# Loading eight decay rates as a column and spreading them over the partitions by a TensorE transpose

## The chip, the cores and the metric

The kernel runs on one core of one Trainium2 chip. A core has a matrix engine (TensorE, PE in the profile), a vector engine (VectorE, DVE), an activation engine (ScalarE, ACT), a general engine (GpSimd, POOL) and a queue engine (SyncE, SP), each with an instruction stream of its own; they meet through semaphores. SBUF and PSUM have 128 partitions, and TensorE writes only into PSUM. The metric is device time in microseconds, the median of several runs; lower is better.

## The reference

A gated linear attention over four sequences of 768 tokens with eight heads is followed by a mixture of eight experts that picks one expert for each token. Only the first part concerns the change:

```python
Dmask = np.where(rel >= 0, lam[:, None, None] ** rel[None, :, :], 0.0)
lam_pow = lam[:, None, None] ** (pos[None, :, None] + 1)
...
intra = np.einsum('bhic,bhjc->bhij', qb, kb) * Dmask[None]
intra = np.einsum('bhij,bhjd->bhid', intra, vb)
inter = np.einsum('bhid,bhde->bhie', qb * lam_pow[None], kv_state)
out[:, :, sl] = intra + inter
rev_pow = lam[:, None, None] ** (block - 1 - pos[None, :, None])
kb_dec = kb * rev_pow[None]
kv_state = lam_block[None, :, None, None] * kv_state + np.einsum('bhsd,bhse->bhde', kb_dec, vb)
```

`lam` holds eight numbers, one decay rate to a head. Everything that the attention multiplies by is a power of them: the causal mask, the powers for the queries, and the reversed powers for the keys. The second part scores each token for the experts and, where a local gate says so, lets it keep its predecessor's expert; then `out = p[e] * relu(x @ w1[e]) @ w2[e]`.

## The kernel before

The attention takes 24 steps, one for each of six chunks of 128 tokens in each of four sequences (`ORDER`, the sequences inside). Step s works on a tile `inp[s]` of 128 partitions by 4 by 512 numbers: transposed queries, transposed keys, values and keys. Six such tiles are held at a time (`LOADS`). The first five are loaded in halves (queries and keys, then values and keys) on SP's queue, in the order tile 0 first half, tile 1 first half, tile 0 second half, tile 1 second half, then both halves of tiles 2 to 4. Later tiles are loaded whole, once TensorE has read the last of the tile six steps before.

A step has these parts. `scores(s)` (L212, or L204 in some steps) multiplies keys by queries into `ps` on TensorE; DVE multiplies the result by `mask` into `sm` (L216). From the second chunk on `from_state(s)` (L239) applies the carried state `kv` to `qd`, queries times powers, which POOL made (L181). `mix(s)` (L252) multiplies values by `sm`, and ACT copies the result to `xc` (L255). `update(s)` (L266) multiplies `kd`, keys times reversed powers, made by POOL (L184), by the values; DVE adds it to `kv` (L269, L271). Between these stand the routing of earlier tokens and the writes of finished rows.

The experts' part follows. It begins with three tiles of 128 tokens that are already known, and then takes the experts one after the other, with TensorE products on weights that SP loads ahead.

The order on TensorE, DVE, SP and POOL is that of the code (`tc.manual_schedule`); ACT's instructions at the start are ordered by a scheduler.

At the very start, `lamb` (L104) is loaded on ACT's queue: each of the 128 partitions gets a copy of all eight rates, read 128 times from DRAM. POOL builds the identity matrix `ident`. TensorE does ten warming products of `ident` with itself, whose result is not used (L874, `WARM`). `masks_of_lam` makes the powers. `spread` (L131) writes one rate into each of 127 columns of a piece, for the even heads on DVE and for the odd heads on ACT; two scans on DVE (L146) multiply along the columns, restarted by ones that come from `ident`, and give `mask`; `rev` (L149) is a column of it. The query powers `lamq` come later from a third spread on ACT and two more scans (L159).

Of the kernel before, what the change touches and what calls it, by code (L numbers as in the profile page):

```python
# [8 lines left out]
F32 = mybir.dt.float32  # L9
# [14 lines left out]
P = 128  # L24
B, H, S, DH = 4, 8, 768, 64
A = H // 2
DM = H * DH
# [13 lines left out]
QUARTERS = [16, 17, 18, 19]  # L41
WIDE = [3, 4, 5, 7, 9, 11]
TURNED = {**{r: r + 1 for r in range(3 * B)}, 11: 13, 20: 22, 21: 23, 22: 23}
WARM = 10
KA = 3
assert KA <= -(-(NA * P - E * (P - 1)) // P)

# [21 lines left out]
def kernel(  # L69
# [9 lines left out]
    nc = tc.nc  # L79
    const = ctx.enter_context(tc.tile_pool(name="const", bufs=1))  # L80
# [19 lines left out]
        return w2[bass.ds(e, 1)].rearrange("o (t p) d -> p (o t) d", p=P)  # L100


    lamb = const.tile([P, H], F32, name="lamb")
    nc.scalar.dma_start(out=lamb, in_=lam.unsqueeze(0).broadcast_to([P, H]))  # L104
    wgt = const.tile([P, DT, EP], F32, name="wgt")
    ident = const.tile([P, P], F32, name="ident")
    make_identity(nc, ident)
# [2 lines left out]

    pg = ctx.enter_context(tc.tile_pool(name="pg", bufs=1, space=PSUM))
    x_ctx = ExitStack()
    load = x_ctx.enter_context(tc.tile_pool(name="load", bufs=LOADS))
    att = x_ctx.enter_context(tc.tile_pool(name="att", bufs=2))
    pows = x_ctx.enter_context(tc.tile_pool(name="pows", bufs=1))
# [754 lines left out]
    with tc.manual_schedule(engines={PE, DVE, SP, POOL}):  # L870

        warm = pg.tile([P, A, P], F32, name="pk0")
        for _ in range(WARM):
            nc.tensor.matmul(warm[:, 0], lhsT=ident, rhs=ident, start=True, stop=True)  # L874
        masks_of_lam()
        nc.gpsimd.memset(wgt, 0.0)
# [453 lines left out]
    with tc.manual_schedule(engines={PE, DVE, SP, ACTE}):  # L1330
        last, i = KA - 1, (KA - 1) % 2
# [121 lines left out]
```

## Time and profile before

| what | before |
|---|---|
| median of 3 runs | 416.93 us (415.94 to 417.92) |
| the profiled execution's own time | 416.13 us |
| its span, first to last instruction | 414.4 us |
| instructions | 10134 |
| PE / DVE / ACT / POOL busy | 96% / 75% / 52% / 44% |
| moved by DMA | 90.69 MB, mean 219 GB/s |
| warming products (L874) | 1.96 to 6.59 us |
| issue of `lamb`, first use of it | 0.82 us, 5.93 us |

Rows of the profile read as follows. In a timeline a row gives the start, the length, the engine, the line, the operation, the tile written and those read, shapes (partitions by elements), the count of entries that were merged, and in brackets the idle time before it with what ended it. "PEld" is the loading of TensorE's stationary operand; "SPq" and "ACTq" are queues that issue DMAs. One product of 32-bit numbers is two entries on TensorE. In a row of DMA queues stand packets, megabytes and the share of the 16 DMA engines' time; q1 is SP's queue, q10 ACT's. In a row of stretches stand the stretch, its length, each engine's busy time (PE, PEld, DVE, ACT, POOL), the granted TensorE clock, the DMA share and GB/s. In a row of groups stand the count, the busy time in us, and the mean of one in ns.

### The profile page before, as it was taken

The page shows a single profiled execution, that of the slowest core. Times are in us where ns is not written, and L with a number is a line of the kernel's source. Part 1 is how long each engine was busy: PE and PEld are TensorE (multiplying, and loading weights), DVE is VectorE, ACT ScalarE, POOL GpSimd, SP SyncE. Part 2 cuts the span into 40 slices and gives each one's busy share as a digit, 9 for nine tenths or more (in the row PEclk, how much of TensorE's full clock was granted, in tenths as well). Part 3 has the DMA queues.
Part 4 walks back from the last instruction along what each step waited for, and adds up shares of the span by engine and source line. Part 5 has one row for each costly group of instructions (what it writes and reads, how often), then busy time and mean ns, then how long its engine had stood idle before and what let it go on. Part 6 is the DMA issues. An engine that isn't in the chain of part 4 may idle for free. (4 is left out here: it accounts for less than half of the span.)

```text
span 414.4 us, 10134 instructions
## 1 busy us (share of the span) xinstructions
PE 397.0 (96%) x3970; PEld 363.4 (88%) x3970; DVE 309.3 (75%) x573; ACT 214.7 (52%) x646; POOL 184.2 (44%) x188
## 2 busy tenths in 40 slices
PE   7999979889999989999999999999999999999994
PEld 6778868667786769989999999999999999999983
DVE  4676987887667797897797786787967868676931
ACT  4245546432931856925944946764674493652210
POOL 4585665440016210147257238617527713700752
PEclk9999999999999999999999999999999999999999
DMA  7999999999987993563464453725617535200111
GB/s 266 404 390 331 361 408 276 331 382 407 355 312 282 361 359 137 219 220 125 197 223 131 173 186 115 270 78 190 235 52 240 179 137 174 96 11 2 43 35 62
DMA packets 36585, 90.69 MB, mean 219 GB/s; under 512 B 3808, under 2 KB 11504, under 8 KB 34608
## 3 DMA queue, kind: packets, MB, share of 16 engines
q1 hardware_dynamic: 30080, 74.47, 49.6%
q0 software_dynamic: 5152, 13.38, 9.7%
q10 hardware_dynamic: 1296, 2.10, 1.3%
q8 instruction: 33, 0.54, 0.5%
q14 instruction: 24, 0.20, 0.1%
HBM read 81.55 MB, written 12.91 MB: 228 GB/s over the span
## 5 line engine op out<-in xcount | busy, mean ns | idle before, releaser
L1122 POOL DMA_INDIRECT out_dram<-yq,sidxq x80 | 93.4, 1167 | 102.5 <-DVE yq L1117 68.1
L1074 PE MATMUL ps<-arena,s 128*128 128x148 f32 (+7 forms) x384 | 63.4, 308 | 2.1 <-DVE part L1240 0.8
L1074 PEld LDWEIGHTS ps<-arena,s 128*128 128x128 f32 x384 | 57.2, 190 | 3.2 <-DVE part L1240 1.2
L777 POOL DMA_INDIRECT xg<-x_dram,gidx x27 | 31.7, 1174 | 55.1 <-DVE xlast L791 16.4
L798 ACT COPY arena<-xlast 32x128 f32<-32x128 f32 x128 | 37.8, 295 | 8.8 <-DVE xlast L791 6.2
L1074 PE MATMUL ps<-arena,w 128*128 128x148 f32 (+7 forms) x256 | 41.9, 307 | 0.0
L1074 PE MATMUL po<-arena,w 128*128 128x148 f32 (+7 forms) x256 | 41.9, 307 | 0.0
L1074 PEld LDWEIGHTS ps<-arena,w 128*128 128x128 f32 x256 | 38.3, 190 | 0.5 <-issue 0.5
L1074 PEld LDWEIGHTS po<-arena,w 128*128 128x128 f32 x256 | 38.2, 190 | 0.0
L216 DVE TENSOR_TENSOR sm<-ps,mask 128x512 f32<-128x512 f32 x46 | 29.4, 680 | 11.2 <-PE ps L212 6.5
L181 POOL TENSOR_TENSOR qd<-inp,lamq 128x512 f32<-128x512 f32 x20 | 25.5, 1277 | 26.4 <-DMA inp<-in_qkv_dram 10.7
L798 ACT COPY arena<-lg 32x128 f32<-32x128 f32 x120 | 35.5, 296 | 2.6
L1112 PE MATMUL pk<-h,w 128*128 128x148 f32 (+6 forms) x224 | 35.1, 310 | 0.0
L1112 PE MATMUL pk<-hsum,s 128*128 128x148 f32 (+6 forms) x224 | 35.1, 310 | 0.0
L1112 PEld LDWEIGHTS pk<-hsum,s 128*128 128x128 f32 x224 | 33.4, 190 | 0.0
L1112 PEld LDWEIGHTS pk<-h,w 128*128 128x128 f32 x224 | 33.4, 190 | 0.0
L252 PE MATMUL po<-sm,inp 128*64 128x128 f32 x384 | 27.8, 280 | 1.4 <-DVE sm L216 0.6
L252 PEld LDWEIGHTS po<-sm,inp 128*64 128x64 f32 x384 | 21.0, 136 | 9.1 <-issue 5.9
L1093 ACT COPY arena<-xlast 32x128 f32<-32x128 f32 x88 | 26.8, 305 | 1.9
L243 ACT ACTIVATE kv<-kv,lamq 128x64 f32<-128x64 f32 x64 | 17.1, 336 | 19.7 <-PE po L239 19.2
L184 POOL TENSOR_TENSOR kd<-inp,rev 128x512 f32<-128x512 f32 x20 | 21.8, 1094 | 9.4 <-DVE rev L149 4.7
L255 ACT COPY xc<-po 128x256 f32<-128x256 f32 x48 | 15.6, 375 | 17.8 <-PE po L252 16.7
(296 smaller groups left out, 750.8 us busy)
## 6 DMA issues: line engine op xcount, KB each, us to landing
w<-in_w_dram SPq DMA_DIRECT2D x23, 2048.0 KB, 9.2
inp<-in_qkv_dram SPq DMA_DIRECT2D x15, 1024.0 KB, 10.8
inp<-in_qkv_dram SPq DMA_DIRECT2D x10, 512.0 KB, 8.1
x_dram<-w SPq DMA_DIRECT2D x12, 256.0 KB, 5.5
inp<-in_qkv_dram SPq DMA_DIRECT2D x4, 768.0 KB, 9.1
x_dram<-xn ACTq DMA_DIRECT2D x8, 256.0 KB, 5.6
w<-in_w_dram SPq DMA_DIRECT2D x4, 512.0 KB, 8.3
out_dram<-yq,sidxq POOLq DMA_INDIRECT x80, 3.1
```

The source lines that it names most:

```text
L181: nc.gpsimd.tensor_tensor(qd, x[:, 0].rearrange("p (a i) -> p a i", i=P), lamq, ALU.mult)
L184: nc.gpsimd.tensor_tensor(kd.rearrange("p (h d) -> p h d", d=DH), x[:, 3].rearrange("p (h d) -> p h d", d=DH), rev.unsqueeze(2).broadcast_ ...
L216: nc.vector.tensor_tensor(sm[:, u], ps[u], mask[:, u], ALU.mult)
L243: nc.scalar.mul(kv[:, a], kv[:, a], lamq[:, a, P - 1:P])
L252: nc.tensor.matmul(head(a, u), lhsT=vn[:, a, u], rhs=sm[:, u, a], start=(not c and a < 2), stop=True, skip_group_check=True)
L255: nc.scalar.copy(xc[:, i::2, b], po[i])
L777: nc.gpsimd.indirect_dma_start(out=xg, out_offset=None, in_=x_dram[:n, :], in_offset=bass.IndirectOffsetOnAxis(ap=gidx[i][:, j:j + 1], axi ...
L798: copy((xt(k) if callable(xt) else xt)[QP * j:QP * j + QP, :, at(k):at(k) + QP], blocks[QP * k:QP * k + QP, :, j])
L1074: nc.tensor.matmul(to[:, j], lhsT=a[:, k, P * m:P * m + P], rhs=b[:, k], start=(new and not j and not k), stop=(k == 1), skip_group_check= ...
L1093: nc.scalar.copy(xu[QP * j:QP * j + QP, u % 2::2 - u % 2, :, P + QP // 2 * k:P + QP // 2 * k + QP // 2], blocks[QP * k:QP * k + QP, :, j]. ...
L1112: nc.tensor.matmul(to[:, m], lhsT=a[:, f, P * m:P * m + P], rhs=b[:, f], start=(new and not m and not f), stop=(f == FT // 2 - 1), skip_gr ...
L1122: last = nc.gpsimd.indirect_dma_start(out=out.rearrange("n (j d) -> (n j) d", j=4), out_offset=bass.IndirectOffsetOnAxis(ap=sidxq[:, u, i, ...
```

## The change

The rates are loaded as a column, `lamc`: eight partitions with one number each. `lamb` becomes the first eight columns of a bank in PSUM. TensorE fills it with one transpose: `lamc`, repeated over 128 columns, against an 8 by 8 identity gives every partition all eight rates. The warming products are five instead of ten, and the transpose stands after the second of them.

```diff
-WARM = 10
+WARM = 5
+EARLY = 2
...
-    lamb = const.tile([P, H], F32, name="lamb")
-    nc.scalar.dma_start(out=lamb, in_=lam.unsqueeze(0).broadcast_to([P, H]))
+    lamc = const.tile([H, 1], F32, name="lamc")
+    nc.scalar.dma_start(out=lamc, in_=lam.unsqueeze(1))
...
+    lamb = pg.tile([P, DM], F32, name="pk1")[:, :H]
...
         warm = pg.tile([P, A, P], F32, name="pk0")
-        for _ in range(WARM):
+        for i in range(WARM):
+            if i == EARLY:
+                nc.tensor.transpose(lamb, lamc.broadcast_to([H, P]), ident[:H, :H])
             nc.tensor.matmul(warm[:, 0], lhsT=ident, rhs=ident, start=True, stop=True)
```

Line numbers after the change are two to four higher. On TensorE the program begins as follows, before; `pk_158` is the bank of the warming products, `ps_111` and `ps_112` receive the first scores:

```order
L1449 UNCONDITIONAL_BRANCH
L874 MATMUL pk_158<-ident 128x128 x10
L212 MATMUL ps_111<-inp 64x128
L212 MATMUL ps_112<-inp 64x128
L212 MATMUL ps_111<-inp 64x128
```

And now, with `pk_89` the bank that holds the rates and `pk_159` that of the warming products:

```order
L1453 UNCONDITIONAL_BRANCH
L878 MATMUL pk_159<-ident 128x128 x2
L877 MATMUL pk_89<-ident,lamc 128x8
L878 MATMUL pk_159<-ident 128x128 x3
L214 MATMUL ps_112<-inp 64x128
L214 MATMUL ps_113<-inp 64x128
```

The transpose stands between the second and the third warming product, and it waits for the load of `lamc`; the first scores follow after three more products. Behind them TensorE's order is as it was.

On ACT the program begins as follows, before:

```order
L104 DMA lamb<-in_lam_dram 128x8
L131 ACT_TABLE_LOAD
L131 COPY w_1_77<-lamb 128x4x127
L152 COPY lamp<-lamb 64x4 x2
L131 COPY w_1_77<-lamp 128x4x127
L154 COPY w_1_77<-lamp 128x4
L361 CAST identb<-ident 128x128
L373 CAST dupq<-ident 128x512
L359 CAST count<-w_1_77 128x32
L360 CAST whole<-w_1_77 128x32
L365 CAST countb<-w_1_77 128x128
L368 CAST beforeb<-w_1_77 128x128
```

And now:

```order
L105 DMA lamc<-in_lam_dram 8x1
L363 ACT_TABLE_LOAD
L363 CAST identb<-ident 128x128
L361 CAST count<-w_1_77 128x32
L362 CAST whole<-w_1_77 128x32
L367 CAST countb<-w_1_77 128x128
L133 COPY w_1_77<-pk_89 128x4x127
L154 COPY lamp<-pk_89 64x4 x2
L370 CAST beforeb<-w_1_77 128x128
L133 COPY w_1_77<-lamp 128x4x127
L156 COPY w_1_77<-lamp 128x4
L371 CAST parts<-whole 128x24
```

Four casts of constants now stand ahead of ACT's spread. The spread reads PSUM, and in the built program it waits for DVE's spread, which reads the same bank, where it waited for the load before. DVE's order is unchanged but for its spread, which reads `pk_89` instead of `lamb` and waits for TensorE instead of the load. POOL's and SP's orders are unchanged.

## The prediction

> **What bounds the kernel now.** The page's busy shares come first, then the last pieces of the span, then its first 25 us.
>
> ```profile
> PE 397.0 (96%) x3970; PEld 363.4 (88%) x3970; DVE 309.3 (75%) x573; ACT 214.7 (52%) x646; POOL 184.2 (44%) x188
> 407.22 1.89 PE L1079 MATMUL pk<-w,hsum 128*128 128x256 f32 x8
> 409.15 0.42 DVE L1200 TENSOR_TENSOR s<-pk,s 128x256 f32<-128x256 f32 x1 [1.30 <-PE pk L1079]
> 409.85 0.98 POOL L827 DMA_INDIRECT out_dram<-s,sidx  x1 [0.74 <-POOLq L1402]
> ```
>
> TensorE (PE) is busy for 96% of the span, and the end is its last product, one VectorE (DVE) addition and the scatter. Whatever moves TensorE's whole program earlier moves the end. The change touches only the start, so the question is how much earlier TensorE gets through it, and whether that lead survives.
>
> ```profile
> 0.82 6.53 SPq L882 DMA_DIRECT2D inp<-in_qkv_dram  x10
> 0.82 0.40 ACTq L104 DMA_DIRECT2D lamb<-in_lam_dram  x1
> 1.96 4.63 PE L874 MATMUL pk<-ident 128*128 128x128 f32 x20 [1.96 <-POOL ident masks.py:199]
> 5.93 0.61 ACT L131 COPY w<-lamb 128x508 f32<-128x508 f32 x1 [3.38 <-DMA lamb<-in_lam_dram]
> 5.93 0.42 DVE L131 COPY w<-lamb 128x508 f32<-128x508 f32 x1 [3.40 <-DMA lamb<-in_lam_dram]
> 6.39 2.34 DVE L146 TENSOR_TENSOR_SCAN mask<-w 128x512 f32<-128x512 f32 x2
> 6.53 1.78 PE L212 MATMUL ps<-inp 64*64 64x128 f32 x32
> 8.76 0.17 DVE L149 COPY rev<-mask 128x8 f32<-128x8 f32 x1
> 8.84 1.28 DVE L216 TENSOR_TENSOR sm<-ps,mask 128x512 f32<-128x512 f32 x2
> 9.02 2.04 POOL L184 TENSOR_TENSOR kd<-inp,rev 128x512 f32<-128x512 f32 x2 [4.68 <-DVE rev L149]
> 9.58 0.43 PE L252 MATMUL po<-sm,inp 128*64 128x128 f32 x2 [0.40 <-DVE sm L216]
> ```
>
> Two chains meet at 8.84, the first `sm`. The mask chain: the decay rates land at 5.93, then spread copy, two scans, `rev`: 2.91 us. The score chain: ten warming products (20 entries, two to a product) hold TensorE until about 6.5, then scores(0) runs to 6.53 + 1.78 = 8.31. The mask is later by half a microsecond, and TensorE then stands idle for `sm` until 9.58. So **the rates' landing at 5.93 is what ends last here**, and the warming products are second by only 0.5 us: an edit that takes away one without the other would be worth no more than that.
>
> From there on the steps hang together without slack:
>
> ```profile
> 15.92 1.16 PE L204 MATMUL ps<-inp 64*128 64x128 f32 x16
> 17.11 1.29 DVE L216 TENSOR_TENSOR sm<-ps,mask 128x512 f32<-128x512 f32 x2 [0.73 <-PE ps L204]
> 17.90 1.64 PE L252 MATMUL po<-sm,inp 128*64 128x128 f32 x16 [0.21 <-issue]
> ```
>
> Scores, mask product, mix, next scores: each starts when the one before ends. A lead at 8.84 is handed on from step to step.
>
> **The change, part by part.** *The load.* `lamb` was 128 rows of eight numbers; `lamc` is eight rows of one. When would it land?
>
> ```profile
> DMA to landing us min/median/max: 5.1/5.1/5.1
> q10 hardware_dynamic: 144, 0.00, 2.1%
> q10 hardware_dynamic: 34, 0.00, 1.3%
> q1 hardware_dynamic: 180, 0.67, 74.6%
> q1 hardware_dynamic: 374, 1.37, 103.1%
> ```
>
> The first row is `lamb`. The next two count packets on ACT's queue (q10), from 2.25 to 5.5 us and from 2.25 to 3.5; the last two count SP's queue (q1), from 2.25 to 5.5 and from 5.5 to 8.75. All 144 packets of `lamb` (128 rows and 16 more) had gone by 5.5, and it landed 0.4 later. Eight rows are at most one per DMA engine, so `lamc` is over after about the first two rounds of 16 packets, which had gone by 3.5. Estimate: 3.5 + 0.4 = **3.9**. Bounds: 3.3, if the first round is enough; 5.9, if a landing in this crowded start takes the time that `lamb` took whatever its size. I take 3.9, since the packets of q10 were spread evenly over the time and the landing followed the last of them.
>
> *The transpose.* It stands behind two warming products, which end at 1.96 + about 0.95 = 2.9, so it waits for `lamc`; behind it in TensorE's queue wait three warming products and scores(0), and nothing else of TensorE's can pass. Its duration is not in the trace; the nearest rows:
>
> ```profile
> L874 PE MATMUL pk<-ident 128*128 128x128 f32 x20 | 4.6, 429 | 2.0 <-POOL ident masks.py:199 2.0
> L454 PE MATMUL pr<-identb,run 4*128 4x4 bf16 x6 | 0.6, 166 | 0.0
> L787 DVE COPY xt<-pr 128x512 f32<-128x512 f32 x1 | 0.7, 692 | 0.1
> ```
>
> Between 0.17 (a tiny product, later on) and 0.43 (a warming one); it is narrow but runs at the slow early pace, so I take 0.35 with the signal. The rates stand in PSUM at 3.9 + 0.35 = **4.25**.
>
> *The mask chain.* DVE's spread now reads PSUM: the copy out of `pr` costs 0.69 for 512 columns, against 0.42 from SBUF: +0.27. The scans and `rev` are as before, so `sm` can start 2.91 + 0.27 = 3.18 after 4.25, at **7.43**. ACT's spread now waits for DVE's instead of running beside it: 4.25 + 0.69 + 0.61 = 5.55, and the second scan, which needs it, starts at about 4.25 + 0.7 + 1.17 = 6.1. Hidden with 0.5 to spare; without that cover it would cost up to 0.6. ACT's constant casts are shuffled around its spread, and their cover is the time in which ACT idled before its first `xc` copy:
>
> ```profile
> 11.09 0.65 ACT L255 COPY xc<-po 128x256 f32<-128x256 f32 x2 [1.28 <-PE po L252]
> ```
>
> That copy moves up with mix(0); so does the spread ahead of it, and the 1.28 stays.
>
> *The score chain.* Three warming products are six entries at (4.63 - 0.42) / 19 = 0.22: 1.33, from 4.25 to 5.6. Scores(0) then also needs the first half tile of q and k:
>
> ```profile
> q1 hardware_dynamic: 145, 0.56, 68.0%
> q1 hardware_dynamic: 293, 1.10, 77.6%
> inp<-in_qkv_dram SPq DMA_DIRECT2D x1, 512.0 KB, 6.6
> ```
>
> Its 144 packets (128 rows and 16) had gone by 5.1 (first row: 1.75 to 5.1); the second half tile's, 288 in all, by 6.4 (second row). It landed about 0.6 later, so the first is there at about 5.7, perhaps sooner without q10's packets. Scores(0): 5.7 + 1.78 = **7.5**. The two chains meet again, mask 7.43, scores 7.5, against 8.84: **1.3 us earlier**. Bounds: 2.0, with `lamc` at 3.3 and q and k sooner, and 0.5 or less, with `lamc` from about 4.8 on. The third half tile (issue near 1.7, 6.6 to landing: 8.3) carries v and the second k; mix(0) wants it at about 8.2, `kd` at once. No more than 0.1 is lost: mix(0) waits for the second half of `sm` until 7.5 + 1.28 = 8.8 anyway, and `kd`(0), half of the 2.04 above, ends at 9.4 while mix(0) still runs.
>
> **Does the lead last?** The loads run at the queue's full rate for the first 60 us, so they will not all come sooner.
>
> ```profile
> 12.00:24.00 12.00, 11.26 (x198) 8.47 (x196) 8.09 (x15) 3.90 (x13) 7.06 (x6) 1.00 1.04 409
> 48.00:60.00 12.00, 11.05 (x264) 8.78 (x257) 10.54 (x26) 6.41 (x22) 7.53 (x7) 1.00 1.00 400
> 37.48 1.28 POOL L181 TENSOR_TENSOR qd<-inp,lamq 128x512 f32<-128x512 f32 x1 [3.41 <-DMA inp<-in_qkv_dram]
> 39.51 0.90 PE L212 MATMUL ps<-inp 64*64 64x128 f32 x32
> 52.90 1.28 POOL L181 TENSOR_TENSOR qd<-inp,lamq 128x512 f32<-128x512 f32 x1 [3.07 <-DMA inp<-in_qkv_dram]
> 53.89 0.43 PE L212 MATMUL ps<-inp 64*64 64x128 f32 x3
> ```
>
> The DMA share (the last number but one) is 1.04 and 1.00. Tile 14 landed at about 52.8 by `qd`, and its scores began at 53.89: 1.1 us of slack, the smallest that I find; tile 10 (37.4 and 39.51) has 2.0, nearer to the rest. A lead of 1.3 would overrun it by 0.2, unless the loads gain as much at the start, where q1 moved 0.67 MB in the 3.25 us beside `lamb` and 1.37 in the next 3.25. I count no loss. Later stages hang on TensorE, and the lead reaches the end.
>
> Sum: 416.13 (the profiled execution: 414.4 of span and 1.7 around it) - 1.3 = 414.8. The median of the runs, 416.93, lies 0.8 above that execution; by it the forecast is **415.6**.
>
> **Rivals.** *The loads take part of it back* (gain 0 to 0.9, 416.0 to 416.9): q1 does not speed up, tile 14 is 0.2 or more late, or q and k land after 5.7. For it: the DMA share of 1.0. Against it: the 2.0 us of tile 10.
>
> *The loads gain as well* (gain 1.9 to 2.8, 414.1 to 415.0): if the 144 packets were what halved q1's rate, q1 gains up to 0.7 MB at 1.37 / 3.25 = 0.42 MB a microsecond, 1.7 us, and with `lamc` at 3.3 the start gains 2.0. Against it:
>
> ```profile
> q1 hardware_dynamic: 10, 0.04, 46.5%
> ```
>
> From 1.75 to 2.25, before any packet of q10, SP's ten took 0.465 x 16 x 0.5 / 10 = 0.37 us each; from 5.5 to 8.75 it was 1.031 x 16 x 3.25 / 374 = 0.14. They were slow without `lamb` beside them.
>
> *The warm pace comes later.* The rows:
>
> ```profile
> 6.50:8.00 1.50, 1.47 (x28) 1.47 (x32) 1.00 1.00 410
> 8.10:9.10 1.00, 1.00 (x40) 0.83 (x32) 1.00 0.98 401
> ```
>
> The same products (L212) took 1.47 / 28 = 0.053 us each before 8.0 and 1.00 / 40 = 0.025 after, with a granted clock of 1.00 in both: TensorE doubles its pace about 6 us after its first product. Now it stands idle from 2.9 to 3.9. If the doubling wants unbroken work, it starts anew at about 4.2, and comes 2.2 us later, at 10.2; from 8.0 on TensorE then works at half pace for 2.2, losing 1.1 of the 1.3: gain 0.2, **416.7**. Against it: until 8.7 the mask product, not TensorE, sets the pace. The Trainium skill, "TensorE: Matmul & The Clock Gate", section "Part 1: The HAM clock gate (the "warmup" mystery)", says that the array runs at half clock until one free-running window of 3.4 us was busy. By it the doubling could slip a whole window, an estimate of 1.7 lost and 417.3, or not at all if the next window begins after 4.2; the trace agrees with the half pace, though not in its clock column.
>
> *`lamc` lands late, or no sooner than `lamb`.* TensorE now waits for it too: scores(0) ends 0.35 + 1.33 + 1.78 = 3.46 after its landing, so beyond 8.84 - 3.46 = 5.4 the kernel is **slower**, us for us. At `lamb`'s own 5.9 it is 0.5 slower, 417.4; at 8.3, as the third half tile, 2.9 slower, 419.8. For it: every packet was slow in these microseconds. Against it: 34 packets of q10 had gone by 3.5.
>
> **How the numbers follow.** Forecast (gain 0.9 to 1.9) 0.53; loads take part back 0.15; loads gain as well 0.12; warm pace later 0.11; late landing 0.09. The range, 414.0 to 417.4, reaches from the load gain to the late landing's near end and leaves out its far end and some scatter (the runs before spread over 2.0 us). A measurement of this kernel can tell about 0.5%, 2.1 us, from no change. The load gain and the upper edge of the forecast give 0.20 for faster by more than that; slower needs a landing past 7.5: 0.04; within it 0.76.
>
> **What would show it.** `lamc` landing near 3.9 and the transpose right behind it; DVE's spread near 4.3 and 0.69 long; ACT's spread done before the second scan; scores(0) at about 5.7; the first `sm` at about 7.5; tile 14's scores near 52.6. It is wrong if `lamc` lands after 5, if the products after 8 us keep the slow pace, or if TensorE waits for tiles near 50 us.

## The result, and the profile after

| | median us | lowest to highest | runs |
|---|---|---|---|
| before | 416.18 | 413.74 to 418.70 | 20 |
| after | 414.02 | 412.00 to 416.64 | 20 |

The ratio is 0.9948, with a 95% interval of 0.9931 to 0.9964: a gain of 2.16 us, between 1.5 and 2.9 by the interval. The profiled execution took 415.91 us with a span of 414.2, against 416.13 and 414.4 before; within either set of 20 the executions scatter by up to 5 us, so those two totals say nothing. What can be read in a trace is where the lead arises and which wait ends last. In the experiments below the microseconds are the median of all executions, while the ratio leaves out the slow ones, those over 1.5% above the fastest of their kernel, and is not exactly the ratio of the two medians.

The start of the changed kernel in order of time (start, duration, engine, line, operation, count; in brackets the idle time before it and what ended it):

```profile
0.82 0.58 ACTq L105 DMA_DIRECT2D lamc<-in_lam_dram  x1
1.96 1.22 PE L878 MATMUL pk<-ident 128*128 128x128 f32 x4 [1.96 <-POOL ident masks.py:199]
3.11 0.27 PE L877 MATMUL pk<-ident,lamc 8*128 8x8 f32 x1
3.31 1.65 PE L878 MATMUL pk<-ident 128*128 128x128 f32 x6
3.42 0.69 DVE L133 COPY w<-pk 128x508 f32<-128x508 f32 x1 [0.90 <-PE pk L877]
4.14 0.58 ACT L133 COPY w<-pk 128x508 f32<-128x508 f32 x1 [0.69 <-DVE w L133]
4.14 2.34 DVE L148 TENSOR_TENSOR_SCAN mask<-w 128x512 f32<-128x512 f32 x2
4.89 1.59 PEld L214 LDWEIGHTS ps<-inp 64*64 64x64 f32 x32 [0.22 <-DMA inp<-in_qkv_dram]
4.89 1.99 PE L214 MATMUL ps<-inp 64*64 64x128 f32 x32
6.52 0.17 DVE L151 COPY rev<-mask 128x8 f32<-128x8 f32 x1
6.94 1.29 DVE L218 TENSOR_TENSOR sm<-ps,mask 128x512 f32<-128x512 f32 x2 [0.25 <-PE ps L214]
8.36 1.09 PE L254 MATMUL po<-sm,inp 128*64 128x128 f32 x16
14.55 1.16 PE L206 MATMUL ps<-inp 64*128 64x128 f32 x16 [0.28 <-DMA inp<-in_qkv_dram]
```

The transpose at 3.11 has no DMA named in its bracket: the rates were there before the two products ahead of it had ended. The first `sm` begins at 6.94 instead of 8.84, a lead of 1.90, and now it waits for TensorE's scores, which had themselves waited for q and k (0.22 in the row of the weight loading at 4.89), no longer for the mask, which was ready at 6.52 + 0.17 = 6.69. From there the lead changes from step to step: 1.22 at mix(0) (8.36 instead of 9.58), which TensorE reaches only when scores(0) and, behind them, scores(1) are done (their last products begin at 8.15), and 1.37 at the scores of tile 3 (14.55 instead of 15.92), whose row names a wait for that tile's DMA.

The queues of the same kernel in the stretches that were shown of before (packets, MB, share of 16 engines), first ACT's from 1.75 to 2.25 us, then SP's from 2.25 to 5.5 and from 5.5 to 8.75:

```profile
q10 hardware_dynamic: 16, 0.00, 1.6%
q1 hardware_dynamic: 286, 1.07, 98.6%
q1 hardware_dynamic: 301, 1.09, 93.6%
```

All of ACT's 16 packets are over by 2.25. SP's queue moves 1.07 MB where it moved 0.67, and then 1.09 where it moved 1.37. Over both stretches together it is 2.16 against 2.04 MB: the first tiles come sooner, the later ones hardly.

### The profile page after: what moved, and what is told of

The parts are those of the page before. It is cut to its first block, busy times and chain, and to the rows that moved or that the text cites. A ratio compares the mean times of both kernels' runs of the same rounds, so it can differ in the third digit from the quotient of the medians.

```text
span 414.2 us, 10116 instructions
## 1 busy us (share of the span) xinstructions
PE 396.3 (96%) x3961; PEld 362.3 (87%) x3961; DVE 310.3 (75%) x573; ACT 214.7 (52%) x646; POOL 183.5 (44%) x188
```

## The experiments

They ran in three sets; all kernels of a set share the runs of the kernel before. The first set ran on a chip on which the kernel before took 424.22 us (35 runs), the other two on a chip on which it took 415.67 (35 runs) and 416.38 (34 runs). "Lead" is how much earlier than in the kernel before the scores of tile 3 begin in the profiled execution (15.92, and 15.95 in the repeat).

### Nothing changed, and the change again

The kernel before against itself, for the scatter of such a comparison, and the changed kernel a second time.

> The kernel before, unchanged, against itself. In the first four runs two kernels came out 0.2 to 0.7% slower than their first sm would have it (e2 had it 0.4 us earlier than before, and was 0.6% slower). Theory M with scatter (a kernel's time also holds waits for instructions that have nothing to do with the change): the ratio may miss 1.000 by more than its interval says, up to 0.3%. Rival (the differences are of the kernels): 1.000 within 0.1%.

Measured: 416.54 us, ratio 1.0019 (0.9985 to 1.0053).

> The changed kernel, unchanged, in the same call. M: the first sm at 6.9 again, the time 0.995 to 0.997 of before. Rival (the gain seen first was mostly scatter): 0.998 to 1.002.

Measured: 414.53 us, ratio 0.9972 (0.9938 to 1.0006), so a gain of 1.2 us here, and a lead of 15.95 - 14.63 = 1.32. In order of time:

```profile
4.89 1.49 PE L214 MATMUL ps<-inp 64*64 64x128 f32 x32
6.61 1.28 DVE L218 TENSOR_TENSOR sm<-ps,mask 128x512 f32<-128x512 f32 x2
8.43 1.09 PE L254 MATMUL po<-sm,inp 128*64 128x128 f32 x16 [0.94 <-DMA inp<-in_qkv_dram]
14.63 1.16 PE L206 MATMUL ps<-inp 64*128 64x128 f32 x16 [0.21 <-DMA inp<-in_qkv_dram]
```

Here scores(0) took 1.49 instead of 1.99, since TensorE doubled its pace sooner, and `sm` began 0.33 earlier than in the first profile. It brought nothing: mix(0) then waited 0.94 for the second half of tile 0 and began at 8.43 against 8.36. **That load is the next bound of the start**, here and in the kernel with the transpose first, below. A null comparison that reads 1.0019 also says how far a single ratio is to be trusted: to about 0.3%.

### One part alone: fewer products

```diff
 (the kernel before)
-WARM = 10
+WARM = 5
```

> The kernel before with five warming products instead of ten, the rates still loaded as 128 rows. Theory M (two chains meet at the first sm: the mask chain from the rates' landing, the score chain from the warming products; both must be shortened): scores(0) start at about 5.7 instead of 6.5, but the mask is still ready at 8.84, so the first sm stays at 8.8 to 8.9 and the time within 0.1% of before. Theory W (the gain of the change comes from having fewer products): first sm about 1 us or more earlier, time 0.995 of before. Theory L (it comes from the rates' packets no longer slowing the first tiles): no change.

Measured: 425.69 us, ratio 1.0033 (0.9994 to 1.0071). Every theory had put it at 1.001 or less, which the interval still holds.

> The kernel before with five warming products, a second time on another chip. Two-chains theory: the mask still waits for the rates near 6, the first mask product stays at 8.8 to 9.0, ratio 0.998 to 1.002. Rival, that the fewer products cost time (the 1.0033 of the first time): 1.002 to 1.005.

Measured: 416.01 us, ratio 0.9985 (0.9959 to 1.0012). The trace of the second, in order of time:

```profile
1.96 2.50 PE L874 MATMUL pk<-ident 128*128 128x128 f32 x10 [1.96 <-POOL ident masks.py:199]
5.88 1.98 PE L212 MATMUL ps<-inp 64*64 64x128 f32 x32 [1.42 <-DMA inp<-in_qkv_dram]
6.04 0.42 DVE L131 COPY w<-lamb 128x508 f32<-128x508 f32 x1 [3.52 <-DMA lamb<-in_lam_dram]
8.96 1.28 DVE L216 TENSOR_TENSOR sm<-ps,mask 128x512 f32<-128x512 f32 x2
16.03 1.16 PE L204 MATMUL ps<-inp 64*128 64x128 f32 x16
```

TensorE gets free at 4.46 and waits until 5.88 for q and k; the mask still ends last, `sm` stays at 8.96, and the lead is -0.1 (-0.4 in the first set). By itself this part moves nothing at the start. And it shows when q and k land beside the old load: at about 5.9, against 4.89 or sooner with the new one.

### One part alone: the eight rates and the transpose

```diff
 (the changed kernel)
-WARM = 5
+WARM = 10
```

> The changed kernel with ten warming products again, the transpose after the second. M: the mask is ready at about 6.6, but scores(0) start at about 6.8 and end near 8.7, so the first sm is at 8.6 to 8.9 and the time within 0.1% of before. W: no change. L: the tiles come as early as in the changed kernel, so most of its gain is kept, 0.995 to 0.997.

Measured: 427.34 us, ratio 1.0061 (1.0021 to 1.0101).

> The changed load and transpose with ten warming products, a second time on another chip. Two-chains theory: the first mask product near 8.4 behind the scores, a lead of about 0.4 at scores(3), ratio 0.998 to 1.001. Rival, that the load and the transpose without the fewer products cost time (the 1.0061 of the first time): 1.004 or more.

Measured: 415.66 us, ratio 0.9987 (0.9956 to 1.0018). The trace of the second:

```profile
6.52 0.17 DVE L151 COPY rev<-mask 128x8 f32<-128x8 f32 x1
6.88 1.10 PE L214 MATMUL ps<-inp 64*64 64x128 f32 x32
8.05 1.29 DVE L218 TENSOR_TENSOR sm<-ps,mask 128x512 f32<-128x512 f32 x2 [1.35 <-PE ps L214]
15.13 1.16 PE L206 MATMUL ps<-inp 64*128 64x128 f32 x16
```

The mask is ready at 6.69, and DVE waits 1.35 for TensorE, which the products hold until 6.88. The lead is 0.8 in this execution, in which the pace doubled early, and 15.92 - 15.49 = 0.43 in that of the first set, where scores(0) began at 7.03. How close the two chains lie thus depends on the moment of the doubling. In the repeat of the kernel before, where it came early, scores(0) ended at 7.13, and the first `sm` waited for the mask until 8.88, 1.75 later (0.5 in the first profile):

```profile
6.03 1.10 PE L212 MATMUL ps<-inp 64*64 64x128 f32 x32
8.88 1.28 DVE L216 TENSOR_TENSOR sm<-ps,mask 128x512 f32<-128x512 f32 x2
```

Either part alone moves the start by less than a microsecond, both together by 1.3 to 1.4. The total of the first set, 1.0061, does not fit a lead, nor anything that was expected; what that chip adds is told below.

### The transpose elsewhere

```diff
 (the changed kernel: the transpose behind all five products)
         for i in range(WARM):
-            if i == EARLY:
-                nc.tensor.transpose(lamb, lamc.broadcast_to([H, P]), ident[:H, :H])
             nc.tensor.matmul(warm[:, 0], lhsT=ident, rhs=ident, start=True, stop=True)
+        nc.tensor.transpose(lamb, lamc.broadcast_to([H, P]), ident[:H, :H])
```

> The changed kernel with the transpose after all five warming products instead of after two. M: the transpose is at about 4.2 instead of 3.1 and the mask ready at about 7.7, so the first sm is at 7.7 instead of 6.94: 0.8 of the lead is lost at that place, and 0.4 to 0.8 at the end (the third tile's load takes 0.3 of it in the changed kernel anyway): 0.996 to 0.997 of before. L and W: as the changed kernel, 0.995.

Measured: 424.94 us, ratio 1.0034 (0.9997 to 1.0071).

> The changed kernel with the transpose behind all five products, a second time on another chip. Two-chains theory: scores(0) near 4.8, the first mask product near 7.9, a lead of about 1.0 at scores(3), ratio 0.996 to 0.999. Rival, that this order costs time (the 1.0034 of the first time): 1.002 or more.

Measured: 414.28 us, ratio 0.9943 (0.9919 to 0.9966). The trace of the second:

```profile
4.39 0.27 PE L877 MATMUL pk<-ident,lamc 8*128 8x8 f32 x1
7.88 1.28 DVE L218 TENSOR_TENSOR sm<-ps,mask 128x512 f32<-128x512 f32 x2
14.96 1.16 PE L206 MATMUL ps<-inp 64*128 64x128 f32 x16
```

A transpose 1.28 later makes the first `sm` 0.94 later, with the mask last again, and the lead 1.0 in both executions (15.92 - 14.96 in the first set too). The totals of the two sets are 0.9% apart for the same kernel, and both missed what was expected, one on each side: a lead of 1.0 would be 0.9976.

```diff
 (the changed kernel: the transpose ahead of all products)
-EARLY = 2
+EARLY = 0
```

> The changed kernel with the transpose ahead of all five warming products, so that its start shows when the column lands. M as now understood (the column's 16 packets had gone by 2.25 us): the transpose starts at 2.6 to 2.8, the five products end at about 5.0, scores(0) start at 5.0 to 5.2, the first sm is at 7.0 to 7.2, and the time is that of the changed kernel, 0.995 to 0.997 of before. If the column lands only at 3.1, where the transpose started in the changed kernel: transpose at 3.1, first sm at 7.4, 0.996 to 0.998. If it lands at 3.9, as predicted, that would have been seen there.

Measured: 414.69 us, ratio 0.9974 (0.9947 to 1.0002). The trace:

```profile
2.28 0.24 PE L877 MATMUL pk<-ident,lamc 8*128 8x8 f32 x1 [2.28 <-DMA lamc<-in_lam_dram]
5.66 0.17 DVE L151 COPY rev<-mask 128x8 f32<-128x8 f32 x1
6.93 1.29 DVE L218 TENSOR_TENSOR sm<-ps,mask 128x512 f32<-128x512 f32 x2 [1.10 <-PE ps L214]
8.37 1.09 PE L254 MATMUL po<-sm,inp 128*64 128x128 f32 x16 [0.61 <-DMA inp<-in_qkv_dram]
```

This kernel tells when the rates land, since nothing else holds the transpose: **at 2.28**, 1.46 after the issue began. The mask is then ready 0.86 sooner than in the changed kernel, and DVE waits 1.10 for the scores: mix(0) stays at 8.37, where the load ends. The mask is out of the way by a wide margin. The transpose came sooner than the 2.6 to 2.8 that was expected, and the total just missed its range.

### What held SP's queue

The old load of 128 rows, into a tile that nothing reads, behind the load of the eight rates (first kernel) and ahead of it (second):

```diff
+    crowd = const.tile([P, H], F32, name="crowd")
+    nc.scalar.dma_start(out=crowd, in_=lam.unsqueeze(0).broadcast_to([P, H]))
```

> The changed kernel with the old load of 128 rows put back beside the column, into a tile that nothing reads. L: the first tiles are slowed as before, and the whole gain is gone: 1.000. M: the mask is ready at about 6.6 all the same, but the first half tile lands near 5.7 instead of 4.9, so scores(0) end at about 7.5 and the first sm is there, 0.6 later than in the changed kernel: 0.996 to 0.997. W: as the changed kernel, 0.995.

Measured: 422.66 us, ratio 0.9955 (0.9921 to 0.9990), a lead of 15.92 - 14.42 = 1.50, so nothing is lost. SP's and ACT's queue from 2.25 to 5.5 us:

```profile
q1 hardware_dynamic: 271, 1.01, 85.9%
q10 hardware_dynamic: 80, 0.00, 1.4%
```

None of the 128 rows moved before 3.5, where 34 packets had gone in the kernel before. From 3.5 to 5.5 SP's queue moved 0.73 MB beside 80 of them, 0.76 in the changed kernel beside none, and 0.44 in the kernel before beside 110. So the rows as such don't slow the tiles, and both expectations that they do fell, the later first half tile (scores(0) began at 4.90) and the lost gain. That left their place on the queue:

> The changed kernel with the old load of 128 rows (into a tile that nothing reads) ahead of the load of the eight rates on ACT's queue. Position theory: 128 rows halve SP's queue only where they are issued together with SP's first load at 0.82, as before the change; so SP's queue moves about 0.67 MB between 2.25 and 5.5 us again (1.01 to 1.07 without), and the rates, second on the queue, land at about 4 to 6, the first mask product begins at 8.5 or later, ratio to the kernel before 0.998 to 1.004. Rival, that the rows' place does not matter and SP's queue was slow for another reason: SP moves about 1.0 MB, scores(0) begins at 4.9 after a transpose that waits for the rates only, ratio 0.994 to 0.998.

Measured: 416.46 us, ratio 0.9999 (0.9972 to 1.0027). The same two queues in the same stretch, and then the trace:

```profile
q1 hardware_dynamic: 148, 0.57, 70.5%
q10 hardware_dynamic: 135, 0.00, 1.9%
```

```profile
5.99 0.27 PE L879 MATMUL pk<-ident,lamc 8*128 8x8 f32 x1 [2.81 <-DMA lamc<-in_lam_dram]
7.77 1.99 PE L216 MATMUL ps<-inp 64*64 64x128 f32 x32
9.82 1.29 DVE L220 TENSOR_TENSOR sm<-ps,mask 128x512 f32<-128x512 f32 x2 [0.25 <-PE ps L216]
16.90 1.16 PE L208 MATMUL ps<-inp 64*128 64x128 f32 x16
```

Issued at 0.82, together with SP's first load, the same 128 rows cut SP's queue to 0.57 MB; issued 0.61 later, behind the eight rates, they leave it 1.01. So it is the rows issued first that the change took out of the tiles' way; whether the moment counts or the place ahead of the other load is not separated, and why the first moments decide over the next three microseconds is not shown. This kernel is also the prediction's late landing in the flesh: rates at 5.99, scores(0) held back until 7.77, tile 3's scores 0.95 later than in the repeat of the kernel before (the prediction's sum gives 5.99 + 3.46 - 8.84 = 0.6). The total does not resolve a loss of that size.

### Does a lead reach the end?

```diff
 (the changed kernel)
-WARM = 5
+WARM = 20
```

> The changed kernel with fifteen more warming products behind the transpose, to see whether a delay at the first sm lasts to the end. They put scores(0) at about 9.8 and the first sm near 10.8, 3.8 us later than in the changed kernel and about 2 later than in the kernel before; mix(2) at about 16, 1.6 later than before. M (steps hang together without slack): the time is 3 us or more above the changed kernel's and 1.5 to 2.0 above that of before, 1.004 to 1.005. Rival (the loads set the pace of the first 60 us, and a delay at the start only uses up their lead): within 0.1% of before.

Measured: 417.97 us, ratio 1.0037 (1.0003 to 1.0071). The trace has:

```profile
18.32 1.16 PE L206 MATMUL ps<-inp 64*128 64x128 f32 x16
```

Tile 3's scores begin 18.32 - 14.63 = 3.69 later than in the repeat of the changed kernel, and the medians of the two differ by 417.97 - 414.53 = 3.4 us, give or take some 2 by their two intervals. A delay at the start comes out at the end nearly whole. That a lead does is not the same thing, since a lead can run into loads that have not landed, and a delay can't.

Between, the shift is hidden under other things. The starts of three milestones in the profiled executions (tile 3's scores; the first product of the experts' part, `ps<-arena`; the end of TensorE's work):

| kernel | tile 3's scores | first `ps<-arena` | TensorE's end |
|---|---|---|---|
| before | 15.92 | 148.05 | 409.11 |
| before, again | 15.95 | 148.25 | 409.20 |
| after | 14.55 | 147.51 | 408.57 |
| after, again | 14.63 | 146.91 | 407.96 |
| transpose first | 14.57 | 148.59 | 409.65 |
| transpose last, second set | 14.96 | 144.98 | 406.04 |
| before with five products, second set | 16.03 | 149.69 | 410.75 |

From the second milestone to the third every row has 261 us; all scatter arises between the first two, whose distance goes from 130.0 to 134.0. At the end the changed kernel is thus 0.5 us ahead in the first pair of profiles and 1.2 in the second. In the first profile of the changed kernel the large waits on the way are such rows:

```profile
60.81 0.98 PE L254 MATMUL po<-sm,inp 128*64 128x128 f32 x14 [0.69 <-issue]
73.45 0.65 PE L241 MATMUL po<-qd,kv 64*64 64x128 f32 x10 [1.51 <-issue]
80.70 0.69 PE L268 MATMUL pk<-inp,kd 128*64 128x64 f32 x16 [1.65 <-DVE kv L271]
```

The third is a wait of an update for DVE near 80 us. It is 1.0 to 2.0 us long in six rows of the table and absent from the one with 130.0. The first two have no releaser in the profile. The kernel before has such waits too (0.88 at 55.20, 1.27 at 61.60), at other places in each execution; as sums of 2.8 to 4.3 us they do not by themselves follow the distances, which are 130.0 and 134.0 where both sums are 4.0. The profile does hold a trace of what they wait for. A queue of its own, q8, of the kind "instruction", moves single packets of 0.02 MB, here in the stretch from 58 to 59 us (and one from 71 to 72):

```profile
q8 instruction: 1, 0.02, 6.5%
```

All thirty waits without a releaser of 0.6 us or more between 40 and 92 us, in the traces of this document, end 2.2 to 2.6 us after the profile counts such a packet, though not every packet is followed by one. So TensorE probably waits for its own program there; no run tests it.

On the chip of the first set there were more waits without a releaser, in the experts' part and not behind packets of q8, here in the changed kernel with ten products:

```profile
327.44 1.99 PE L1078 MATMUL ps<-arena,s 128*128 128x186 f32 x8 [2.33 <-issue]
```

From its first to its last `ps<-arena` the part took 256.57 us in that kernel and 255.83 in the one with the transpose last; in the kernel before, on the chip of its profile, it took 245.76. No trace of the kernel before was kept from the chip of the first set, so what made the totals of 1.0061 and 1.0034 there stays open. On the other chip the intervals of the same kernels hold what their leads would give, but for the transpose last: its 0.9943 (0.9919 to 0.9966) is more than a lead of 1.0 accounts for, and its profiled execution is the one with the shortest middle part.

## Why the prediction was right, and where its sizes were off

*What bounds the kernel: right.* The rates' landing ended last and the products were second. It is the leads at tile 3 that show it, -0.4 and -0.1 for the fewer products, 0.4 and 0.8 for the load and the transpose, 1.3 to 1.4 for both; the totals (0.9985 and 0.9987 for the parts on the chip of the later sets, 0.9972 for the whole there) have overlapping intervals. The distance of 0.5 between the chains was that of one execution: with an early doubling it is 1.75, and one part alone was then worth 0.8, more than the 0.5 that the prediction allowed it.

*The landing: mis-sized.* Predicted 3.9 with bounds of 3.3 to 5.9; measured 2.28, outside the bounds. The step that failed is the one that had the packets of q10 spread evenly over the time and eight rows done after two rounds of 16 by 3.5. Of the 144 packets of `lamb` none had gone by 2.25, and 34 by 3.5; the 16 of `lamc` were all over by 2.25, so the pace of the one load did not price the other. It did not matter for the sum, since the transpose stands behind two products, which ended at 3.11, not 2.9.

*The transpose and the mask chain: right.* From 3.11 to the start of DVE's spread it is 0.31 (0.35 predicted), the spread took 0.69 as predicted, and from there to the end of `rev` it is 6.69 - 3.42 = 3.27 (3.18). ACT's spread ended at 4.14 + 0.58 = 4.72, well ahead of the second scan, which starts halfway through the two scans of 2.34, at about 5.3: 0.6 to spare, where the prediction had 0.5.

*The score chain: mis-sized.* The first half tile of q and k was put at about 5.7, perhaps sooner without q10's packets. They were there by 4.89, and "perhaps sooner" was 0.8 us. From the first of the three products to scores(0) it is 4.89 - 3.31 = 1.58, not 1.33, since the weight loading ahead of scores(0) still waited 0.22 for q and k: the load, not the products, held scores(0), as the prediction had it, but at an earlier time. Both chains together gave the first `sm` 1.90 of lead (2.27 in the repeat, 8.88 - 6.61) instead of 1.3.

*The third half tile: mis-sized the other way.* No more than 0.1 was to be lost to it. With the first `sm` earlier than reckoned, mix(0) was no longer held by `sm`: in the first profile the scores ahead of it held it, and in the repeat, with faster scores, it waited 0.94 for the load, which ended at about 8.4, close to the 8.3 that the prediction gave it. These, and waits of 0.2 to 0.3 at tile 3, bring the lead back to 1.3 to 1.4, near the predicted 1.3: two errors that cancel, not a term that was right.

*The loads gain as well: half of it was right.* The prediction counted against this rival that SP's packets were slow before any of q10's. That stayed so (10 packets from 1.75 to 2.25, as before). But from 2.25 on the rows issued first were the cause of the half rate, and 0.40 MB more were moved in the first stretch. The rival's price of 1.7 us needed that gain to stay, and 0.28 MB of it were given back in the next. Tile 14 shows the end of it, in order of time the changed kernel's first profile and then its repeat:

```profile
52.90 1.28 POOL L183 TENSOR_TENSOR qd<-inp,lamq 128x512 f32<-128x512 f32 x1 [3.24 <-DMA inp<-in_qkv_dram]
53.97 0.90 PE L214 MATMUL ps<-inp 64*64 64x128 f32 x32
```

```profile
52.77 1.26 POOL L183 TENSOR_TENSOR qd<-inp,lamq 128x512 f32<-128x512 f32 x1 [3.85 <-DMA inp<-in_qkv_dram]
52.95 0.56 PE L214 MATMUL ps<-inp 64*64 64x128 f32 x12
```

The tile lands when it did before, at 52.8 to 52.9. The slack of 1.1 is still there in the first, in which other waits had eaten the lead by then, and 0.2 is left in the repeat. No product of TensorE waited for it, so "no loss" held, but the next microsecond of lead would be lost there.

*The warm pace comes later: its condition never came.* The rival wanted TensorE idle ahead of the transpose, and with the rates at 2.28 it was not. Where TensorE does pause, the runs bear the rival out. In the second run of the kernel before with five products (idle from 4.46 to 5.88) the products of mix(0), in windows (length, then TensorE's busy time and count):

```profile
10.00:10.30 0.30, 0.30 (x3) 0.01 (x1) 1.00 1.06 437
10.30:10.60 0.30, 0.30 (x7) 0.30 (x8) 1.00 1.08 437
```

The pace doubles at about 10.3, 4.4 after TensorE resumed. With the 128 rows first, idle from 3.19 to 5.99, it doubles at 10.4, again 4.4 after. Without a pause it doubled between 5.4 and about 8.8, so 3.4 to 6.8 after the first product. The latest is the kernel with twenty products, which in windows of half a microsecond is still at the slow pace at 8.0 and at the fast one at 9.0:

```profile
8.00:8.50 0.50, 0.50 (x4) 0.50 (x4) 1.00 1.08 442
9.00:9.50 0.50, 0.50 (x7) 0.50 (x6) 1.00 1.02 418
```

Counted from the resumption the 4.4 lie within that span. The Trainium skill, "TensorE: Matmul & The Clock Gate", section "Part 1: The HAM clock gate (the "warmup" mystery)", says that the window of 3.4 us is free-running, so that the moment differs from run to run; the traces agree, though the column of the granted clock (the last number but two) stays at 1.00 through it. The warming products thus do have a use, to keep TensorE from pausing; five of them are enough because q and k now land by 4.89, with a pause of 0.2 at most.

*The total.* Predicted a gain of 1.3, measured 2.16 (1.5 to 2.9) and, on the second occasion, 1.2 (-0.2 to 2.6). The traces show a lead of 1.3 to 1.4 at tile 3, of 0.5 and 1.2 at TensorE's end, and nothing beyond it that stays. Whether the first comparison's further 0.8 is more than the scatter of such a comparison (1.0019 for a kernel against itself) remains open. It is this remainder that carried the gain to the edge of 2.1 us, for which, and beyond, the prediction gave 0.20.

## What to carry to other kernels

Where two chains meet, price them together: the halves of this change led by -0.1 and 0.8 us in the trace and read 0.9985 and 0.9987, not to be told from nothing, and the whole led by 1.3 to 1.4; afterwards a third thing, here a load that nobody had waited for, sets the place. A small transfer that is cut into many rows can cost another queue's loads more than itself: issued together with SP's first load the 128 rows took about 0.4 MB from it in 3.25 us, and behind the eight rates next to nothing. And a lead of one or two microseconds is to be read at a fixed place in the trace, since the totals of single executions scatter by more.

## What the runs showed of the hardware

- The load of eight numbers to eight partitions landed 1.46 us after its issue began, of which ACT spent 0.58 on the issue; that of 128 rows, to 128 partitions, took 5.1.
- 128 rows of 32 bytes, issued at the same moment as another queue's first load, left that queue 0.57 to 0.67 MB in 3.25 us; issued 0.61 later behind another small load, 1.01 (1.02 to 1.08 without them).
- TensorE's pace for these products doubled 3.4 to 6.8 us after its first product without a pause, and 4.4 us after a pause of 1.4 or 2.8 us; the granted clock's column shows neither.
- TensorE's waits of 0.6 us or more without a releaser, between 40 and 92 us, ended 2.2 to 2.6 us after a packet on the queue q8 ("instruction").
- One chip took 2% longer for the same kernel (424.22 against 415.67 and 416.38), with waits of up to 2.3 us on TensorE, in the experts' part, that have no releaser in the profile.
